# Reading the moving operand of the gate, value and output products from its last column to its first

## The chip, the cores and the metric

The kernel runs on one core of one Trainium2 chip. The metric is the device time of one execution in microseconds (us), the median of several runs. A change of 0.2% is 1.5 us here.

## The reference

An attention through 32 packed queries per head feeds a gated feed-forward layer. Eight batches of 576 positions, eight heads of 64, model width 512, inner width 1536; all data are float32.

```python
def sm_attn(qq, kk, vv):
    s = scale * np.matmul(qq, kk.transpose(0, 1, 3, 2))
    s = s - np.max(s, axis=-1, keepdims=True)
    a = np.exp(s)
    a = a / (np.sum(a, axis=-1, keepdims=True) + 1e-09)
    return np.matmul(a, vv)
p_packed = sm_attn(p, k, v)          # 32 rows per head
out = sm_attn(q, p_packed, p_packed) # 576 rows per head
...
x = out.transpose(0, 2, 1, 3).reshape(B * S, H * D)
g = x @ w_gate
silu = g * (1.0 / (1.0 + np.exp(-g)))
val = x @ w_val
return silu * val @ w_out
```

## The kernel before

**Stages.** For each batch `b` the first attention gives the 32 packed rows per head (`s1_...` for the first two batches, `q_...` from the third), the second attention gives the softmax weights of the 576 queries over the 32 packed rows (`s2_...`). The attention output itself is never formed. The packed rows are multiplied into the two weight matrices instead (`m_mm`, through `by_head` at L267), and the result, tile `m`, holds for one pair of 128-column blocks of the inner width what 128 (head, packed row) pairs contribute. The softmax weights stand transposed in tile `a2`: 128 partitions, two groups of heads, 576 query columns.

**Gate and value.** `gv_chunk` (L621) makes one block `fc` (0 to 11) of 128 inner columns for one chunk of queries. A batch has two chunks, A of 256 queries (`NA`) and B of 320 (`NB`); in even batches A comes first in the columns of `a2`, in odd batches B does. The stationary operand of each product is a 128x128 slice of `m`, the moving operand is the chunk's columns of `a2`, and the result in PSUM (tile `gv`) has the inner columns on partitions and the queries in its 256 or 320 columns. Both operands are split into a high and a low part in the type float32r, so that each product is three matmuls (low x high, high x low, high x high) for two head groups: six for the gate (`s` = 0), six for the value (`s` = 1), at L635.

**Output.** ScalarE takes the gate through SiLU (L642), VectorE multiplies it with the value (L646; the 64 queries of a chunk B beyond 256 go to tile `t4` at L649), and the product is split again into `hh` and `hl` (L178, L616). `out_mm` (L652) then takes 128 of these queries as stationary operand and a 512-column block of `w_out` as moving operand, in three parts (`hl` x `wo_h`, `hh` x `wo_l`, `hh` x `wo_h`, L654), and adds over the twelve `fc` in four PSUM tiles `acc`. `emit_out` (L662) copies a finished tile to SBUF and stores it with a DMA on SP's queue. After an odd batch the rows gathered in `t4` run through the same products into a tile `aux` (`behind_p4`, L963).

**Batch 0.** It runs from a list of words written out by hand (`PROGRAM`), beside the conversion of the weights from their 64-bit form. Its gate and value products are at L787, its output products at L828. For the first two weight tiles (`PLAIN`) and the first five pairs of `w_out` (`SPLIT`) it uses plain float32 operands, with one matmul per product in the code; the profile shows each of these as two.

**Order.** The steps of the next batches' attention are put between the products by the tables `FIRST` and `LATER` (`plan_of`, L707): at each place `fill`, `behind` and `between` in `gv_chunk` and `outs` a few of them are issued. TensorE's own order is the order of the code. The host lays the inputs out before the launch: `heads_t` (L991) puts the queries of a batch and head one after another in the order in which they come, `wo` (L1007) holds rows of `w_out` as they are.

Of the kernel before, what the change touches and what calls it, by code (L numbers as in the profile page):

```python
# [20 lines left out]
B, H, S, D = 8, 8, 576, 64  # L21
NP = 32
DM, DF = 512, 1536
P = 128
NPAR, NHP = 2, 4
NFC = DF // P
# [6 lines left out]
NA, NB = 256, 320  # L33
# [99 lines left out]
def tile_pack_attention_swiglu(ctx: ExitStack, tc: tile.TileContext, qT, kT, v, vq, pT, wgv, wout, out):  # L133
# [69 lines left out]
    sts, wos, wo_h, wo_l = {}, {}, {}, {}  # L203
# [58 lines left out]
    def by_head(outs, lhs, rhs):  # L262

        for hp in range(NHP):
            for par in range(NPAR):
                r = slice(64 * par, 64 * par + 64)
                nc.tensor.matmul(outs[par][32 * hp : 32 * hp + 32], lhs(r, hp), rhs(r, hp), start=True, stop=True)  # L267
# [344 lines left out]
    def h_split(src, hi, lo, between=lambda: False, tag=""):  # L612
        hh, hl = (pool.tile([P, 256], F32R, tag=t + tag, bufs=2, name=t) if tag else h_tile(t) for t in ("hh", "hl"))
        copy(hi, hh, src)
        last = between()
        low = lo.tensor_tensor(hl, src, hh.bitcast(F32), op=ALU.subtract)  # L616
        if last:
            pin(low)
        return hh, hl

    def gv_chunk(b, fc, is_b, fill, behind, between):  # L621
        odd = b % 2
        n = NB if is_b else NA
        off = (0 if odd else 256) if is_b else (320 if odd else 0)
        mh, ml = ms[b, fc // 2]
        ah, al = a2[b]
        f = fc % 2
        pgs = []
        for s in range(2):
            pg = ps_gv.tile([P, 512], F32, tag="gv", name="gv")  # L630
            pgs.append(pg)
            i = 0
            for m_, a_ in ((ml, ah), (mh, al), (mh, ah)):
                for g in range(NPAR):
                    nc.tensor.matmul(  # L635
                        pg[:, :n], m_[:, g, f, s * P : (s + 1) * P], a_[:, g, off : off + n],
                        start=(i == 0), stop=(i == 5),
                    )
                    i += 1
            fill()  # L640
        sg = pool.tile([P, NB], F32, tag="sg", bufs=1, name="sg")
        nc.scalar.activation(sg[:, :n], pgs[0][:, :n], AF.Silu)  # L642
        behind()
        hf = pool.tile([P, 256], F32, tag="hf", bufs=2, name="hf")
        o, o4 = (64, 0) if is_b and odd else (0, 256)
        nc.vector.tensor_tensor(hf, pgs[1][:, o : o + 256], sg[:, o : o + 256], op=ALU.mult)  # L646
        if is_b:
            r, r4 = slice(64 * odd, 64 * odd + 64), slice(o4, o4 + 64)
            nc.vector.tensor_tensor(t4[b // 2][:, fc, r], pgs[1][:, r4], sg[:, r4], op=ALU.mult)  # L649
        return h_split(hf, nc.scalar, nc.vector, between)  # L650

    def out_mm(acc, hh, hl, c, fc):  # L652
        for i, (h_, w_) in enumerate(((hl, wo_h), (hh, wo_l), (hh, wo_h))):
            nc.tensor.matmul(  # L654
                acc[:, :],
                h_[:, c : c + P],
                w_[fc // 2][:, fc % 2],
                start=(fc == 0 and i == 0),
                stop=(fc == NFC - 1 and i == 2),
            )  # L660
# [60 lines left out]
    with tc.manual_schedule(engines={mybir.EngineType.PE}):  # L721
# [17 lines left out]
        with tc.manual_schedule(  # L739
# [18 lines left out]
            rows, accs = [], []  # L758
# [13 lines left out]
            held = {}  # L772

            def gv(i):
                fc, is_b = order[i]
                off, n = (NA, NB) if is_b else (0, NA)
                k, f = divmod(fc, 2)
                if k < PLAIN:
                    terms = ((ms[0, k][0], a2fs[0]),)
                else:  # L780
                    (mh, ml), (ah, al) = ms[0, k], a2[0]
                    terms = ((mh, ah), (mh, al), (ml, ah))
                held[i] = [ps_gv.tile([P, 512], F32, tag="gv", name="gv") for _ in range(2)]
                for s in range(2):
                    todo = [(m_, a_, g) for m_, a_ in terms for g in range(NPAR)]
                    for j, (m_, a_, g) in enumerate(todo):
                        nc.tensor.matmul(  # L787
                            held[i][s][:, :n], m_[:, g, f, s * P : (s + 1) * P], a_[:, g, off : off + n],
                            start=(j == 0), stop=(j == len(todo) - 1),
                        )  # L790

            def half(i):
                fc, is_b = order[i]
                if fc // 2 < SPLIT:
                    return h0[fc // 2][:, fc % 2, 256 * is_b : 256 * is_b + 256]
                if i not in hs:
                    hs[i] = [pool.tile([P, 256], F32, tag="hf", bufs=2, name="hf")]
                return hs[i][0]
# [23 lines left out]
            def outs(i):  # L822
                fc, is_b = order[i]
                for c in range(2):
                    if fc // 2 >= SPLIT:
                        out_mm(accs[2 * is_b + c], *hs[i][1:], c * P, fc)
                        continue
                    nc.tensor.matmul(  # L828
                        accs[2 * is_b + c], half(i)[:, c * P : c * P + P], wos[fc // 2][:, fc % 2],
                        start=(fc == 0), stop=(fc == NFC - 1),  # L830
                    )

# [23 lines left out]
            def half_of(f, b):  # L856
# [5 lines left out]

            words = {
                "g": gv, "silu": silu, "h": hmul, "hh": h_high, "hl": h_low, "out": outs,
                "z_scores": lambda x: (None if x else s1_tile(0), s1_scores(0, x)), "z_max": lambda x: s1_max(0, x),
                "z_top": lambda x: s1_top(0), "z_exp": lambda x: s1_exp(0, True), "z_turn": lambda x: s1_turn(0, x),
# [26 lines left out]
        def last_outs(rows, accs, out):  # L893
# [5 lines left out]
            return last  # L899

        behind = last_outs(rows, accs, lambda which: outs(2 * NFC - 2 + which))

        steady[0] = True
        def batch(b, behind):
# [6 lines left out]
            def outs(fc, which, fill=lambda: None):  # L911
                src = (hb if which else ha).pop(fc)
                for c in range(2):
                    out_mm(accs[2 * which + c], *src, c * P, fc)
                    fill()

            for fc in range(NFC):
                count = [0]

                def fill():  # L920
                    count[0] += 1
                    if count[0] == 2:
                        run(fc, 2)
                        if fc == NFC - 1 and b + 1 < B:
                            m_part(b + 1, 0, both)
                        elif fc % 2 and fc + 1 < NFC:
                            m_part(b, (fc + 1) // 2, both)
                    if b == 1 and 1 <= fc <= 2 * SPLIT - 4 and count[0] == 7:
                        wout_high(fc + 3)
                        wout_low(fc + 3)  # L930
                    if count[0] != 2:
                        run(fc, count[0])

                ha[fc] = gv_chunk(b, fc, False, fill, lambda: run(fc, "a"), lambda: run(fc, "ha"))
                m_lows()
                if fc:
                    outs(fc - 1, 0, fill)
                else:
                    behind(0)
                hb[fc] = gv_chunk(b, fc, True, fill, lambda: run(fc, "b"), lambda: run(fc, "hb"))  # L940
                if fc:
                    outs(fc - 1, 1, fill)
                else:
                    behind(1)
                    for x, y in zip((rows, accs), accs_of(b)):
                        x.extend(y)
# [11 lines left out]
            def mm4(*ks):  # L958
                for k in ks:
                    for i in range(2):  # L960
                        out_mm(p4[0], *halves[k], i * P, 2 * k + i)
# [59 lines left out]
```

## Time and profile before

| | |
|---|---|
| median of 3 runs | 735.83 us (735.49 to 736.95) |
| the profiled execution's own time | 736.46 us |
| its span, first to last instruction | 734.7 us |
| TensorE matmul (PE) busy | 725.7 us, 99% of the span |
| weight loads (PEld) busy | 592.0 us, 81% |
| VectorE (DVE) busy | 454.4 us, 62% |
| ScalarE (ACT) busy | 373.9 us, 51% |
| granted TensorE clock, mean | 0.998 |
| DMA, mean over the span | 81 GB/s |

PE's rows are matmuls, PEld's rows the weight loads, which run beside them. A matmul's own duration contains its way through the array, so the durations of successive matmuls overlap. What one matmul costs a stream is therefore the distance from its start to the next one's start. The chain of waits follows the work that ended last back from the last instruction; a row of it in order of time has a start, a stretch in us, the engine, the tile and line, and how many instructions the stretch holds. For a piece with nothing but matmuls in a row, the stretch divided by the count is that distance. Rows of the timeline have start, length, engine, line, operation, operands and shape; equal neighbours are merged, with their count at the end.

### The profile page before, as it was taken

Reading aid. Unit: us, or ns where it says so; the run is one execution under the profiler, and the core shown is the slowest. Engines: PE = TensorE matmul, PEld = TensorE weight load, DVE = VectorE, ACT = ScalarE, POOL = GpSimd, SP = SyncE. Lnnn points to the kernel's source line nnn. Section 1 sums busy time; section 2 is a strip of 40 time slices with the busy share of each in tenths; the row PEclk is TensorE's granted clock in tenths of the full one; section 3 lists DMA queues with packets and bytes.
Section 4 is the critical chain, followed back from the end, with each engine's and each line's share of the span. In section 5 each row is a group of like instructions: output and inputs, shape, how many; then the busy total and the mean of one; then the engine's idle time right before and its main releaser. Section 6 shows DMA issues by size and latency. Waiting matters only on the chain.

```text
span 734.7 us, 15099 instructions
## 1 busy us (share of the span) xinstructions
PE 725.7 (99%) x6242; PEld 592.0 (81%) x6242; DVE 454.4 (62%) x1009; ACT 373.9 (51%) x668; POOL 2.0 (0%) x13
## 2 busy tenths in 40 slices
PE   8999999999999999999999999999999999999997
PEld 4655667888888888888888888888888888888886
DVE  4999779665755557663764646665574555744333
ACT  3789737754635445563563535654453535533331
POOL 0000000000000000000000000000000000000000
PEclk9999999999999999999999999999999999999999
DMA  9697482310112201302112011102001000010001
GB/s 351 249 356 269 145 308 97 117 73 2 65 58 85 74 1 65 127 4 73 66 44 98 15 63 65 40 22 73 1 2 72 4 2 1 1 58 1 1 1 71
DMA packets 20004, 59.15 MB, mean 81 GB/s; under 512 B 5984, under 2 KB 7008, under 8 KB 17376
## 3 DMA queue, kind: packets, MB, share of 16 engines
q1 hardware_dynamic: 19792, 58.12, 21.8%
q8 instruction: 49, 0.80, 0.4%
q14 instruction: 19, 0.16, 0.1%
q10 hardware_dynamic: 144, 0.07, 0.0%
HBM read 48.69 MB, written 9.49 MB: 79 GB/s over the span
## 4 chain that ended last, share of the span: by engine, by line
PE 95%; DVE 1%; issue 0%; DVEq 0%
PE gv L635 36%; PE acc L654 33%; PE aux L267 7%; PE gv L787 6%; PE acc L828 5%; PE aux L654 4%; PE gv_aux L482 1%; PE gv_aux L398 1%; PE gv_aux L267 1%; DVE w L200 0%; PE acc L728 0%; PE aux L343 0%; DVE e L467 0%; DVE w L201 0%; PE aux L324 0%
## 5 line engine op out<-in xcount | busy, mean ns | idle before, releaser
L642 ACT ACTIVATE sg<-gv 128x256 f32<-128x256 f32 (+1 forms) x168 | 69.1, 411 | 176.0 <-PE gv L635 162.0
L646 DVE TENSOR_TENSOR hf<-gv,sg 128x256 f32<-128x256 f32 x168 | 71.0, 423 | 130.2 <-PE gv L635 118.9
L635 PE MATMUL gv<-a2h,ml 128*128 128x256 f32 (+1 forms) x672 | 143.9, 295 | 0.0
L635 PE MATMUL gv<-a2l,mh 128*128 128x256 f32 (+1 forms) x672 | 143.5, 295 | 0.0
L635 PE MATMUL gv<-a2h,mh 128*128 128x256 f32 (+1 forms) x672 | 143.3, 294 | 0.0
L654 PE MATMUL acc<-wo_h,hl 128*128 128x512 f32 x344 | 140.7, 409 | 0.0
L654 PE MATMUL acc<-wo_h,hh 128*128 128x512 f32 x344 | 135.4, 394 | 0.0
L654 PE MATMUL acc<-wo_l,hh 128*128 128x512 f32 x344 | 134.8, 392 | 0.0
L635 PEld LDWEIGHTS gv<-a2h,ml 128*128 128x128 f32 x672 | 116.4, 188 | 15.1 <-ACT sg L803 0.4
L178 ACT CAST hh<-hf 128x256 fp32r<-128x256 f32 x168 | 67.8, 403 | 102.0 <-DVE hf L646 101.9
L635 PEld LDWEIGHTS gv<-a2l,mh 128*128 128x128 f32 x672 | 107.8, 188 | 0.0
L635 PEld LDWEIGHTS gv<-a2h,mh 128*128 128x128 f32 x672 | 107.7, 188 | 0.0
L616 DVE TENSOR_TENSOR hl<-hf,hh 128x256 fp32r<-128x256 f32 x168 | 69.9, 416 | 46.5 <-ACT hh L178 46.4
L654 PEld LDWEIGHTS acc<-wo_h,hl 128*128 128x128 f32 x344 | 64.5, 187 | 27.8 <-issue 19.2
L654 PEld LDWEIGHTS acc<-wo_h,hh 128*128 128x128 f32 x344 | 64.5, 188 | 15.5
L654 PEld LDWEIGHTS acc<-wo_l,hh 128*128 128x128 f32 x344 | 64.7, 188 | 8.1 <-issue 0.2
L569 DVE TENSOR_TENSOR ml<-aux,mh 128x512 fp32r<-128x512 f32 x92 | 59.0, 682 | 5.6 <-ACT mh L599 5.5
L267 PE MATMUL aux<-w,ppt 64*32 64x512 f32 (+1 forms) x784 | 52.1, 588 | 0.9 <-DVE w L201 0.9
L599 ACT CAST mh<-aux 128x512 fp32r<-128x512 f32 x92 | 49.4, 590 | 5.7 <-PE aux L267 1.3
L642 ACT ACT_TABLE_LOAD x30 | 38.5, 1283 | 13.8 <-PE gv L635 10.0
L828 PE MATMUL acc<-wo_f,h 128*128 128x512 f32 x80 | 37.8, 603 | 0.0
L828 PEld LDWEIGHTS acc<-wo_f,h 128*128 128x128 f32 x80 | 14.2, 189 | 16.6 <-issue 16.2
(153 smaller groups left out, 756.6 us busy)
## 6 DMA issues: line engine op xcount, KB each, us to landing
st<-in_wgv SPq DMA_DIRECT2D x12, 1024.0 KB, 5.8
k_t<-in_kT SPq DMA_DIRECT2D x16, 576.0 KB, 4.9
q_t<-in_qT SPq DMA_DIRECT2D x16, 576.0 KB, 4.9
out<-ot SPq DMA_DIRECT2D x36, 256.0 KB, 2.1
v_t<-in_vq SPq DMA_DIRECT2D x6, 1280.0 KB, 5.7
st<-in_wout SPq DMA_DIRECT2D x6, 1024.0 KB, 6.0
v_t<-in_v SPq DMA_DIRECT2D x2, 1024.0 KB, 8.5
p_t<-in_pT SPq DMA_DIRECT2D x7, 64.0 KB, 2.4
```

The lines of the kernel that those rows point to most:

```text
L178: e.copy(dst, src)
L267: nc.tensor.matmul(outs[par][32 * hp : 32 * hp + 32], lhs(r, hp), rhs(r, hp), start=True, stop=True)
L398: nc.tensor.matmul(pss[par][NP * j : NP * j + NP, i * SQ : (i + 1) * SQ], p_t[r, 2 * g + i, :], k_t[r, j // 2, 2 * g + i, j % 2 * SQ : j % ...
L569: pin(nc.vector.tensor_tensor(*lows.pop(0), op=ALU.subtract))
L599: nc.scalar.copy(m[0][at], src)
L616: low = lo.tensor_tensor(hl, src, hh.bitcast(F32), op=ALU.subtract)
L635: nc.tensor.matmul(pg[:, :n], m_[:, g, f, s * P : (s + 1) * P], a_[:, g, off : off + n], start=(i == 0), stop=(i == 5),)
L642: nc.scalar.activation(sg[:, :n], pgs[0][:, :n], AF.Silu)
L646: nc.vector.tensor_tensor(hf, pgs[1][:, o : o + 256], sg[:, o : o + 256], op=ALU.mult)
L654: nc.tensor.matmul(acc[:, :], h_[:, c : c + P], w_[fc // 2][:, fc % 2], start=(fc == 0 and i == 0), stop=(fc == NFC - 1 and i == 2),)
L787: nc.tensor.matmul(held[i][s][:, :n], m_[:, g, f, s * P : (s + 1) * P], a_[:, g, off : off + n], start=(j == 0), stop=(j == len(todo) - 1),)
L828: nc.tensor.matmul(accs[2 * is_b + c], half(i)[:, c * P : c * P + P], wos[fc // 2][:, fc % 2], start=(fc == 0), stop=(fc == NFC - 1),)
```

## The change

A helper `back_to_front` takes an access pattern with one run of columns and returns one that starts at the last column and steps backward by one. It is applied to the moving operand at all four places where the feed-forward products are issued: L635, L654 (L658 in the changed program), L787 (L791) and L828 (L832). The stationary operands and the PSUM tiles keep their patterns. So that the results come out in the same columns, the host lays two inputs out backward: the columns of `w_out`, and the queries of each chunk, so that `a2` holds a chunk's queries in reverse. The host's work is not part of the time.

```diff
-                        pg[:, :n], m_[:, g, f, s * P : (s + 1) * P], a_[:, g, off : off + n],
+                        pg[:, :n], m_[:, g, f, s * P : (s + 1) * P], back_to_front(a_[:, g, off : off + n]),
...
+    def back_to_front(x):
+        (p0, pn), (step, n) = x.ap
+        return bass.AP(x.tensor, x.offset + (n - 1) * step, [(p0, pn), (-step, n)])
+
     def out_mm(acc, hh, hl, c, fc):
...
-                w_[fc // 2][:, fc % 2],
+                back_to_front(w_[fc // 2][:, fc % 2]),
...
-                            held[i][s][:, :n], m_[:, g, f, s * P : (s + 1) * P], a_[:, g, off : off + n],
+                            held[i][s][:, :n], m_[:, g, f, s * P : (s + 1) * P], back_to_front(a_[:, g, off : off + n]),
...
-                        accs[2 * is_b + c], half(i)[:, c * P : c * P + P], wos[fc // 2][:, fc % 2],
+                        accs[2 * is_b + c], half(i)[:, c * P : c * P + P], back_to_front(wos[fc // 2][:, fc % 2]),
...
-    qT, kT = heads_t(q), heads_t(k)
+    backward = [
+        np.r_[n - 1 : -1 : -1, S - 1 : n - 1 : -1] for b in range(B) for n in ((NB if b % 2 else NA),)
+    ]
+    qT, kT = heads_t(np.stack([q[b][:, backward[b]] for b in range(B)])), heads_t(k)
...
-    wo = np.ascontiguousarray(wo).reshape(NFC, P, DM).view(np.int64)
+    wo = np.ascontiguousarray(wo[:, ::-1]).reshape(NFC, P, DM).view(np.int64)
```

The order of the instructions on every engine, their shapes and the semaphores they wait for are the same in both programs, row by row; only the line numbers differ. Of a moving operand only the first address and the sign of the step change: for one product of chunk B the pattern goes from 320 columns from column 256 upward to 320 columns from column 575 downward.

## The prediction

> **What bounds the kernel now.** I read the profile's page first, for which engine is busy and what the chain of waits is made of.
>
> ```profile
> span 734.7 us, 15099 instructions
> PE 725.7 (99%) x6242; PEld 592.0 (81%) x6242; DVE 454.4 (62%) x1009; ACT 373.9 (51%) x668; POOL 2.0 (0%) x13
> PE 95%; DVE 1%; issue 0%; DVEq 0%
> PE gv L635 36%; PE acc L654 33%; PE aux L267 7%; PE gv L787 6%; PE acc L828 5%; PE aux L654 4%; PE gv_aux L482 1%; PE gv_aux L398 1%; PE gv_aux L267 1%; DVE w L200 0%; PE acc L728 0%; PE aux L343 0%; DVE e L467 0%; DVE w L201 0%; PE aux L324 0%
> ```
>
> The chain runs through matmuls for 95% of the span, and 84% of it (36 + 33 + 6 + 5 + 4) is the five groups whose moving operand the change turns round. VectorE and ScalarE stand at 62% and 51%: a few per cent more or less on TensorE passes to the end nearly whole. How often the groups run is in the groups of matmuls with the shapes kept apart, here the three parts of the output products and one gate and value row of each shape (the two other operand pairs have the same counts).
>
> ```profile
> L654 PE MATMUL acc<-wo_h,hl 128*128 128x512 f32 x344 | 140.7, 409 | 0.0
> L654 PE MATMUL acc<-wo_h,hh 128*128 128x512 f32 x344 | 135.4, 394 | 0.0
> L654 PE MATMUL acc<-wo_l,hh 128*128 128x512 f32 x344 | 134.8, 392 | 0.0
> L654 PE MATMUL aux<-wo_h,hl 128*128 128x512 f32 x48 | 18.8, 391 | 0.0
> L635 PE MATMUL gv<-a2h,ml 128*128 128x320 f32 x336 | 76.8, 309 | 0.0
> L635 PE MATMUL gv<-a2h,ml 128*128 128x256 f32 x336 | 67.1, 281 | 0.0
> ```
>
> So 3 x 336 = 1008 products of 256 columns, 1008 of 320, and 3 x (344 + 48) = 1176 of 512: 258,048 + 322,560 + 602,112 = 1,182,720 moving columns in float32r. The mean durations in these rows overlap from one matmul to the next, so the cost of one is taken from the chain in order of time: start, stretch, what, count. First batch 0 with plain float32, then the steady stage, then the tail.
>
> ```profile
> 45.34 2.15 PE gv L787 x8
> 50.00 1.73 PE gv L787 x8
> 55.10 5.15 PE acc L828 x12
> ...
> 655.56 1.42 PE gv L635 x12
> 656.99 1.39 PE acc L654 x6
> 658.38 1.76 PE gv L635 x12
> ...
> 722.74 8.17 PE aux L654 x36
> ```
>
> Divided by the counts: plain float32 takes 2150 / 8 = 269 ns, 1730 / 8 = 216 ns and 5150 / 12 = 429 ns, the last for 512 columns. The timeline tells which shapes the gate and value stretches hold.
>
> ```profile
> 49.84 1.89 PE L787 MATMUL gv<-a2f,mh 128*128 128x256 f32 x8
> ...
> 52.68 2.42 PE L787 MATMUL gv<-a2f,mh 128*128 128x320 f32 x8
> ...
> 655.40 0.40 PE L635 MATMUL gv<-a2h,ml 128*128 128x256 f32 x2
> ```
>
> 216 ns is thus 256 columns, and 269 ns fits 320: (429 - 216) / 256 = 0.832 ns per column and 3 ns per matmul, and 320 x 0.832 + 3 = 269. In float32r the same division gives 1420 / 12 = 118.3 ns for 256 columns, 1760 / 12 = 146.7 for the other chunk's 320, and 1390 / 6 = 231.7 for 512. The slope is (146.7 - 118.3) / 64 = 0.443 ns per column and, from 320 to 512, (231.7 - 146.7) / 192 = 0.443 again; 118.3 - 256 x 0.443 leaves 4.9 ns per matmul. Two things are to be seen. Float32r takes 0.443 ns per column, where half of plain float32's 0.832 would be 0.416: 0.027 ns per column is lost. And the 4.9 ns per matmul is not owed: in the tail 36 products in a row take 8170 / 36 = 226.9 ns each, which is 512 x 0.443 = 226.8 and nothing besides.
>
> **The change part by part.** The added code issues no instruction and takes none away. Order, shapes and waits on each engine stay; DMAs keep their count, bytes and queue, since the host alone lays `q` and `w_out` out anew, which isn't timed. No wait is added, so nothing is queued behind one, and no cover is lost. The results land in the same PSUM columns in the same order of writing, so SiLU (L642), the multiplications (L646, L649), the splits and the stores see the tiles they saw. Each of these edits costs 0, without a range: they have no counterpart on the chip.
>
> What is left is one property: 1,182,720 float32r columns, and those of batch 0, are read at falling addresses. No trace here shows a matmul with a step of -1, so its price is bounded from both sides by the nearest rows.
>
> From above: the slowest rate at which a moving operand of full height is seen to pass is plain float32's 0.832 ns per column. If a falling read of float32r went at that, it would cost (0.832 - 0.443) x 1,182,720 = 460 us more. A nearer bound is that the 0.027 ns per column doubles: 0.027 x 1,182,720 = 32 us more. From below: if the 4.9 ns per matmul went in the 2016 gate and value products and the 1032 output products that aren't in the tail's kind of stretch, 3048 x 4.9 = 14.9 us would go; if the 0.027 ns went too, another 32 us.
>
> I take 0 for it. The loss has the size of a per-column rate that three shapes, two operands (`a2` and `w_out`) and two stages share to the third digit, as a limit does that counts columns or the bytes passed and not the direction. A run of 256, 320 or 512 columns covers the same addresses either way, ends where it began and holds as many words. Batch 0's plain matmuls have 0.416 ns per column to spare before a loss of that size would show at all. That gives 736.46 + 0 = 736.5 us for the profiled execution, which is 0.63 above the median of the three runs; on the median's scale it is 735.8 us.
>
> [...] In the chain 118.3 ns pass for 256 columns while a weight load of 128 columns runs beside each matmul:
>
> ```profile
> L635 PEld LDWEIGHTS gv<-a2h,ml 128*128 128x128 f32 x672 | 116.4, 188 | 15.1 <-ACT sg L803 0.4 <-ACT sg L642 0.3
> ```
>
> [...]
>
> **The rivals.**
>
> Faster: the 4.9 ns are collisions between the moving read and the weight load inside SBUF, and these depend on which addresses the two reads touch at the same moment. Both now rise; with one falling they would cross quickly instead of running along beside each other. For it: the loss comes and goes with the stretch, none in the tail, 4.8 ns (231.7 - 226.9) in the same products of the steady stage, where nothing but the neighbours in the stream is different, so something in the pairing of the reads makes it. Against it: the tail shows that two rising reads can run without it. If all of it goes, 735.8 - 14.9 = 720.9 us; if half, 728.4 us. VectorE and ScalarE have the room to follow.
>
> Slower, the other side: the reader of the moving operand is made for rising addresses, and a falling step costs it more per column, at L635 and L658 alike. Its place is every product of the steady stage; it decides from an extra 1.5 us / 1,182,720 columns = 0.0013 ns per column, a twentieth of the loss that is there. For it: float32r runs at the edge of what the read gives (0.443 against 0.416), so there is no slack to hide even a small extra, while plain float32 has some. Against it: nothing in the trace shows a reader that prefers a direction, all reads of the program being rising. At a third of the present loss it is +10.6 us, 746.4 us; at the whole of it 767.8 us; at plain float32's rate 1196 us.
>
> The change does nothing: this is the forecast itself, and it would look the same if the pattern were turned back into a rising one on the way to the chip; the operands that the trace records for L635 would tell.
>
> **How the numbers follow.** No change within 1.5 us (0.2%, about what a measurement of this kernel can tell from none): 0.38. Faster: 0.36, most of it between a tenth and the whole of the 14.9 us, with 0.04 for more than that. Slower: 0.26, since an unseen operand form without slack is a risk: 0.17 up to half of the doubled loss (+16 us, 752), 0.09 beyond, up to 1196 us. The likeliest case gives 735.8 us; its own range is 734.3 to 737.3. The range for all cases runs from 720, just beyond the whole gain, to 752: it leaves out 0.04 below and 0.09 above.
>
> **What would show it.** Right: the chain's stretches keep 1.42, 1.39 and 1.76 us for 12, 6 and 12 matmuls and 8.17 us for the tail's 36. The faster rival: the 6 products of L658 come to 6 x 226.9 = 1.36 us and the 12 of L635 to 1.36 and 1.70 us, with the tail unchanged. The slower rival: the tail grows too, by the same share per column as the steady stage, and the slope between 256, 320 and 512 columns rises above 0.443 ns while batch 0's 0.832 stays. Wrong altogether: a new wait in the chain on VectorE, ScalarE or a DMA, or a difference in the small attention products (L267, L398, L482), which the change leaves as they are.

## The result, and the profile after

| | before | after |
|---|---|---|
| median | 735.66 us (4 runs, 735.35 to 736.95) | 739.72 us (4 runs, 739.33 to 740.08) |
| the profiled execution's own time | 736.46 us | 739.33 us |
| its span | 734.7 us | 737.5 us |
| granted TensorE clock, mean | 0.998 | 1.000 |

The change makes the kernel slower, by 4.06 us between the medians: the ratio of the runs is 1.0054, with a 95% interval of 1.0042 to 1.0066. The page of the changed kernel has as many instructions on each engine, and the same lines make up the chain.

```profile
PE 728.2 (99%) x6242; PEld 591.9 (80%) x6242; DVE 454.6 (62%) x1009; ACT 373.6 (51%) x668; POOL 2.0 (0%) x13
PE 96%; DVE 1%; issue 0%; DVEq 0%
PE gv L635 36%; PE acc L658 34%; PE aux L267 7%; PE gv L791 5%; PE acc L832 5%; PE aux L658 5%; PE gv_aux L482 1%; PE gv_aux L398 1%; PE gv_aux L267 1%; DVE w L200 0%; PE acc L732 0%; PE aux L343 0%; DVE w L201 0%; PE aux L324 0%; DVE ot L180 0%; PE aux L398 0%
```

PE's busy time grows by 2.5 us, from 725.7; VectorE and ScalarE stay within 0.3 us, and no new engine, line or transfer has as much as 1% of the chain. The loss is inside the matmuls. Their own durations are no measure of it: in the rows of before they are some 162 ns longer than the distance from one to the next at each of the three shapes (281 ns beside 118.3, 309 beside 146.7, 394 beside 231.7). Which of them, the chain in order of time tells (start, stretch, what, count): batch 0 in plain float32, a stretch of 24 `aux` products, three stretches of the steady stage, the last 18 output products and the tail.

```profile
44.45 2.15 PE gv L791 x8
49.10 1.73 PE gv L791 x8
54.20 5.15 PE acc L832 x12
...
558.31 5.60 PE aux L658 x24
...
656.43 1.41 PE acc L658 x6
657.84 1.42 PE gv L635 x12
...
660.66 1.76 PE gv L635 x12
...
721.17 4.20 PE acc L658 x18
725.37 8.41 PE aux L658 x36
```

Two rows of before, for the same stretch of 24 and the last 18 output products:

```profile
556.69 5.45 PE aux L654 x24
...
718.63 4.12 PE acc L654 x18
```

Gate and value stand nearly where they stood, at 1.42 and 1.76 us for twelve; so does batch 0, with 2.15, 1.73 and 5.15. The float32r output products grew: six from 1.39 to 1.41 us, eighteen from 4.12 to 4.20, the tail's 36 from 8.17 to 8.41, which is 226.9 to 233.6 ns each. Over the whole chain, the 158 stretches of six that it holds whole sum to 228.01 us before and 229.94 after, 0.0122 us more for each. The program has 160 of these, which makes 2.0 us. Four stretches of 18 with 0.065 more each make 0.3. The `aux` products come four times 36 at a time: the tail has 0.24 us more, and three times they run as 24 and 12, with 5.60 after 5.45 and 2.81 after 2.76, 0.20 more each time; that makes 0.8. The stretches of twelve gate and value products, taken the same way, come to 1.419 us after 1.414 (256 columns) and 1.763 after 1.762 (320), 0.4 us at 84 of each. Together this is 3.5 us.

The two executions whose rows are shown differ by only 2.87 us (739.33 and 736.46), because the one of before was already 0.9 us late in batch 0: the same stretch starts at 45.34 us there and at 44.45 in the changed kernel. Its granted clock was 0.96 up to there, beside 1.00 in the other. Without that delay the difference is 3.8 us, and the stretches account for nearly all of it.

### The profile page after: what moved, and what is told of

It is laid out like the page before. It is cut to its first block, busy times and chain, and to the rows that moved or that the text cites. A ratio compares the mean times of both kernels' runs of the same rounds, so it can differ in the third digit from the quotient of the medians.

```text
span 737.5 us, 15099 instructions
## 1 busy us (share of the span) xinstructions
PE 728.2 (99%) x6242; PEld 591.9 (80%) x6242; DVE 454.6 (62%) x1009; ACT 373.6 (51%) x668; POOL 2.0 (0%) x13
## 4 chain that ended last, share of the span: by engine, by line
PE 96%; DVE 1%; issue 0%; DVEq 0%
PE gv L635 36%; PE acc L658 34%; PE aux L267 7%; PE gv L791 5%; PE acc L832 5%; PE aux L658 5%; PE gv_aux L482 1%; PE gv_aux L398 1%; PE gv_aux L267 1%; DVE w L200 0%; PE acc L732 0%; PE aux L343 0%; DVE w L201 0%; PE aux L324 0%; DVE ot L180 0%; PE aux L398 0%
## 5 line engine op out<-in xcount | busy, mean ns | idle before, releaser
L635 PE MATMUL gv<-a2h,ml 128*128 128x256 f32 (+1 forms) x672 | 144.2, 296 | 0.0
L635 PE MATMUL gv<-a2l,mh 128*128 128x256 f32 (+1 forms) x672 | 144.0, 296 | 0.0
L635 PE MATMUL gv<-a2h,mh 128*128 128x256 f32 (+1 forms) x672 | 144.0, 296 | 0.0
L658 PE MATMUL acc<-wo_h,hl 128*128 128x512 f32 x344 | 141.6, 411 | 0.0
L658 PE MATMUL acc<-wo_l,hh 128*128 128x512 f32 x344 | 136.8, 398 | 0.0
L658 PE MATMUL acc<-wo_h,hh 128*128 128x512 f32 x344 | 136.7, 397 | 0.0
L635 PEld LDWEIGHTS gv<-a2h,ml 128*128 128x128 f32 x672 | 116.6, 188 | 16.1 <-ACT sg L807 0.4
L635 PEld LDWEIGHTS gv<-a2l,mh 128*128 128x128 f32 x672 | 107.9, 188 | 0.0
L635 PEld LDWEIGHTS gv<-a2h,mh 128*128 128x128 f32 x672 | 107.7, 188 | 0.0
L658 PEld LDWEIGHTS acc<-wo_h,hl 128*128 128x128 f32 x344 | 64.6, 188 | 28.2 <-issue 19.2
L658 PEld LDWEIGHTS acc<-wo_h,hh 128*128 128x128 f32 x344 | 64.7, 188 | 15.7
L658 PEld LDWEIGHTS acc<-wo_l,hh 128*128 128x128 f32 x344 | 64.7, 188 | 8.3 <-issue 0.2
L832 PE MATMUL acc<-wo_f,h 128*128 128x512 f32 x80 | 37.8, 603 | 0.0
L832 PEld LDWEIGHTS acc<-wo_f,h 128*128 128x128 f32 x80 | 14.2, 189 | 16.6 <-issue 16.2
```

What stands on the lines that cost most here:

```text
L635: nc.tensor.matmul(pg[:, :n], m_[:, g, f, s * P : (s + 1) * P], back_to_front(a_[:, g, off : off + n]), start=(i == 0), stop=(i == 5),)
L658: nc.tensor.matmul(acc[:, :], h_[:, c : c + P], back_to_front(w_[fc // 2][:, fc % 2]), start=(fc == 0 and i == 0), stop=(fc == NFC - 1 and ...
L832: nc.tensor.matmul(accs[2 * is_b + c], half(i)[:, c * P : c * P + P], back_to_front(wos[fc // 2][:, fc % 2]), start=(fc == 0), stop=(fc == ...
```

## The experiments

**Which products.** The theory after the result: a falling read costs the output products something, and the gate and value products nothing. The rival: both pay, and the gate and value products hide it behind a gain. Two kernels do one half of the change each; the diffs are against the changed kernel.

```diff
# out_only: back_to_front at L658 and L832 and w_out's columns reversed; the queries stay in order
-  pg[:, :n], m_[...], back_to_front(a_[:, g, off : off + n]),
+  pg[:, :n], m_[...], a_[:, g, off : off + n],
...
# gv_only: back_to_front at L635 and L791 and the queries reversed; w_out stays in order
-  back_to_front(w_[fc // 2][:, fc % 2]),
+  w_[fc // 2][:, fc % 2],
...
```

> Only the output products read w_out back to front; the gate and value products read a2 forward as before. Pairing theory (what changed is how the moving read of an output product meets the weight load beside it): the whole change, 739.7 us against 735.7, since the trace after shows the 512-column products at about 233 to 234 ns and the 256- and 320-column ones as before. Direction theory (a falling step costs a fixed share per column wherever it is): the output products hold 602,112 of the 1,182,720 columns, so about half, 737.7 us.

> Only the gate and value products read a2 back to front; w_out is read forward. Pairing theory: 735.7 us, within 0.5 us of the kernel before, 118 and 147 ns per product. Direction theory: the other half of the columns, about 737.7 us.

The chain's last two stretches, first with the output products alone turned round, then with gate and value alone:

```profile
721.79 4.20 PE acc L658 x18
725.99 8.41 PE aux L658 x36
```

```profile
717.96 4.09 PE acc L658 x18
722.05 8.17 PE aux L658 x36
```

`out_only` takes 739.04 us beside 735.49 for the kernel before, ratio 1.0043 (1.0029 to 1.0056). `gv_only` takes 735.77, ratio 0.9997 (0.9989 to 1.0006). The output products carry the loss. But neither theory holds as put, since something small is hidden in the other half: over the chain of `gv_only`, twelve products of 256 columns take 1.425 us where they took 1.414, 0.9 us at 84 of them, while the forward output products gain about as much, six going from 1.443 to 1.436 on the mean (1.1 us at 160) and the last eighteen from 4.12 to 4.09. Why the output products gain there was not tried.

**One shape at a time.** The next kernel holds nothing but streams of 24 float32r products in a row on one moving operand and two alternating slices of a weight tile, 48 instructions for plain float32. In each pair one stream reads forward (up) and one back to front (down), at various distances in bytes. Distance 0 means that both reads start at the first column of their tiles, which are separate; any other distance moves the weights on by so many bytes (or, in one pair, the moving operand).

```python
for i in range(COUNT):
    nc.tensor.matmul(ps[:, :n], w[:, wo + 256 * (i % 2) : wo + 256 * (i % 2) + P],
                     run(m, mo, n, step), start=(i == 0), stop=(i == COUNT - 1))
```

> No part of the reference: 36 streams of 24 matmuls each, one after another, on one float32r moving tile and two float32r weight slices, with nothing beside them but weight loads. Names with up read the moving tile forward, with down back to front; the letter is the distance in address between weights and moving tile (a 0 bytes, b 256, c 32, d 64, e 128, f 16, g 4, i 96, j 512, k 48; h moves the moving tile by 32 bytes); short has 256 columns, mid 320, the others 512; plain is float32. Pairing theory: up_b, the tail's distance, takes 226.9 ns per matmul and down_b about 233.3; other distances give other values in both directions, and down is not slower than up at all of them. Direction theory: every down is slower than its up by about 6 ns at 512 columns, 3 to 4 at 256 and 320, whatever the distance; both theories: plain 429 ns in both directions.

The chain in order of time; `a` is distance 0, `up_c` 32 bytes, `up_j` 512 bytes, all of 512 columns; `short` is 256 columns, `mid` 320, `plain` 512 in float32:

```profile
14.94 5.44 PE up_a L81 x24
20.38 5.60 PE down_a L81 x24
...
37.05 5.60 PE up_c L81 x24
42.65 5.61 PE down_c L81 x24
...
115.54 5.46 PE up_j L81 x24
...
154.93 3.52 PE mid_up_a L81 x24
158.45 3.52 PE mid_down_a L81 x24
...
169.02 20.60 PE plain_up L81 x48
189.62 20.60 PE plain_down L81 x48
```

Two times for the same product are to be seen: 5440 / 24 = 226.7 ns and 5600 / 24 = 233.3 ns. The forward read has 226.7 to 227.5 only at distances 0, 256 and 512 bytes and 232 to 234 at the eight others; the falling read has 233 or more everywhere. 320 columns take 146.7 ns both ways, and plain float32 doesn't tell the directions apart (20600 / 48 = 429.2 ns both ways). These two times agree with the 226.9 and 233.6 of the kernel's tail.

**Is it the distance?** That suggested a simpler theory: what counts is how the two reads meet, and turning one round only spoils a good meeting. Then a forward read at a bad distance should cost the kernel as much as the change. One padding moves the weights of the output products by 64 bytes, to 192 from a multiple of 256:

```diff
-PAD = 120
+PAD = 104
```

> The kernel before, all reads forward, with the tiles after pp moved down by 64 bytes, so that the weights of an output product lie 192 bytes off a multiple of 256 from its w_out columns instead of on one; nothing else changes. Pairing theory: the same loss as the change without turning any read, the tail at 233.3 instead of 226.9 ns, 738.5 to 739.5 us. Theory that only the falling step costs (at these addresses or anywhere): no change, 735.5 us.

```profile
555.61 5.60 PE aux L654 x24
...
721.76 8.25 PE aux L654 x36
```

It takes 736.10 us beside 735.45, ratio 1.0005 (0.9996 to 1.0014). The three stretches of 24 `aux` products do go to 5.60 us, 233.3 ns a product, which is the falling read's time with every read forward; so the distance can take the better time away in the kernel too. But the tail goes only to 229.2 ns, the stretches of six stay (1.442 us on the mean after 1.443), and the kernel's time moves by 1.0 us at most by the interval: the distance alone is not the cause of the 4 us. That theory fell.

**Does anything give the falling read the better time?** Narrower weights (96, 64 and 32 columns, so that less is read beside the moving operand) and fifteen more distances:

> No part of the reference: streams of 24 matmuls as before. First 512 moving columns with weights of 128, 96, 64 and 32 columns (full, three, half, quarter), forward and back to front, at distance 0; the same with 320 (mid) and 256 (short) moving columns; then back to front with full weights at 15 further distances (down_), and forward at 192, 240, 384 and 512 bytes (up_). Pairing theory: the cost beyond 0.416 ns per column comes from the weight load beside the matmul, so it shrinks with the weight columns: from 233.3 for full to about 225 for half and 220 for quarter back to front. Theory that a falling read costs per column: back to front stays 6.6 ns above forward at all widths. If there is a distance at which the falling read meets no weights, one of the down_ rows shows about 226.7; if not, all show 233.

```profile
14.35 5.44 PE full_up L81 x24
19.79 5.61 PE full_down L81 x24
...
47.66 5.55 PE quarter_up L81 x24
53.21 5.60 PE quarter_down L81 x24
...
78.38 2.72 PE quarter_up_short L81 x24
81.10 2.83 PE quarter_down_short L81 x24
```

The falling 512 columns stay at 233.3 to 236.7 ns at all four widths and all fifteen distances. 256 columns read forward reach 2720 / 24 = 113.3 ns beside narrow weights and 117.9 falling. For 512 columns narrow weights work the other way: the forward read goes from 226.7 ns to 230 or 231. So the falling read's time is its own, while the forward read has a better one that it reaches only at times.

The weights have a part in a forward product's time: over the streams 512 columns take 226.7 to 227.5 or 232 to 234 ns with the weights at different distances, and 256 columns take 113.3 ns beside 32 weight columns where the next run has 2870 / 24 = 119.6 ns beside 128 at the same distance.

**Where 256 and 320 columns have their better time.** If the theory holds for these too, there is a distance at which they gain:

> No part of the reference: streams of 24 matmuls of 256 moving columns, forward (up_) and back to front (down_), with the weights at distances of 0, 16, 32 ... 240 bytes (letters a to p) and of 4 bytes (q). Pairing theory: values between 113 and 121 ns that depend on the distance, with neither direction ahead on average, which is why the gate and value products did not change. Theory that a falling read costs per column: each down_ about 3 ns above its up_.

> Streams of 24 float32r products with no part of the reference: 320 columns read forward at the sixteen distances 0, 16, ... 240 bytes (mod 256) between weights and moving operand (mid_a to mid_p), 256 columns at distances around 64 bytes and at 64 plus one, two, three and four times 256, a few falling ones. Theory A (the rising read has a best rate of 0.4427 ns per column, 226.7 / 512, which it reaches only at favourable distances; the falling read has its own, slower one everywhere): at one or more distances the 320-column stream takes near 320 x 0.4427 = 141.7 ns, at all others 146 to 148; the 256-column stream takes 113.3 at 64 + 256k for every k and 117 to 120 beside it; falling streams 146.8 and 117.8 at every distance, the favourable ones too. Theory B (the 113.3 ns of 256 columns at 64 bytes is a chance of its place in the program, and the fixed 4.9 ns a product are paid by both directions): 320 columns 146 to 148 at all sixteen distances, and 256 columns 117 to 120 at 64 + 256k as well.

In the first kernel `up_a` is distance 0 and `up_e` 64 bytes, 256 columns; in the second `short_c` is 64 bytes and `short_j` 1088 bytes, and `up_again` is `short_c` once more, behind falling streams.

```profile
11.73 2.87 PE up_a L81 x24
...
23.11 2.72 PE up_e L81 x24
```

```profile
73.35 2.74 PE short_c L81 x24
...
92.77 2.72 PE short_j L81 x24
...
118.06 2.83 PE up_again L81 x24
```

256 columns take 113.3 to 114.2 ns, at the least 256 x 0.4427, at 64 bytes and at 64 plus one to four times 256, and 116.7 to 120.4 elsewhere; falling 117.9 to 120.0 at every distance tried. 320 columns stay within 145.8 to 146.7 at all sixteen, so their part of the theory missed. (In `widths` they came to 143.8 forward, beside 32 weight columns.) `up_again` misses too: 117.9 ns at the good distance. So the distance alone doesn't fix a forward read's time; what came before may count too, but no run tries this by itself.

**The good distance in the kernel.** Paddings put every gate and value product 64 bytes from its moving operand, forward and, in a second kernel, with the whole change:

```diff
-                pool.tile([P, NPAR * 4 * P + 24], dt, tag=t, bufs=2, name=t)[:, at : at + NPAR * 4 * P].rearrange(
+                pool.tile([P, NPAR * 4 * P], dt, tag=t, bufs=2, name=t).rearrange(
...
-            t4[b // 2] = pool.tile([P, NFC, P], F32, tag="t4", bufs=1, name="t4")
+            t4[b // 2] = pool.tile([P, NFC * P + 48], F32, tag="t4", ...)[:, : NFC * P].rearrange(...)
...
-        sg = pool.tile([P, NB], F32, tag="sg", bufs=1, name="sg")
+        sg = pool.tile([P, NB + 16], F32, tag="sg", bufs=1, name="sg")[:, :NB]
```

> The kernel before, all reads forward, with the tiles moved by paddings: every float32r gate/value product now has its weights 64 bytes (mod 256) from the start of its moving operand (42 + 84 at the groups' edges 192), where they were spread over thirteen distances; the 869 + 137 out products that stood at distance 0 stay there. Theory A (a rising read reaches its own best rate at the favourable distance, in the kernel as in the streams): the 1058 products of 256 columns go from about 118.2 ns towards the 113.4 ns of the stream, at most 1058 x 4.8 ns = 5.1 us, less what each group of 12 needs to settle; the 1096 of 320 columns stay at 146.7: 731 to 734 us. Theory B (the distance decides only in long streams of one shape): 735.5, as before.

> The same paddings under the changed kernel, all moving operands read back to front. Theory A (the falling read has a rate of its own and finds no favourable distance): 739.7 as without the paddings, 256-column products still 117.6 to 118.5 ns; against the forward kernel with the same paddings the change then costs more than before, 6 to 9 us instead of 4. Theory C (the change costs time only because it alters the distance between the first column read and the weights, and a new distance can mend it): the gate/value products gain as in the forward kernel, 735 to 737.

Last two stretches of the forward kernel, then of the one that reads back to front:

```profile
719.10 4.14 PE acc L656 x18
723.24 8.17 PE aux L656 x36
```

```profile
719.99 4.20 PE acc L660 x18
724.19 8.41 PE aux L660 x36
```

Both misses. Forward takes 736.98 us beside 735.46, ratio 1.0017 (1.0008 to 1.0026): twelve 256-column products went only from 1.414 to 1.408 us where 1.36 was hoped for, and the last eighteen output products, which weren't meant to change, from 4.12 to 4.14, and six of them from 1.443 to 1.448 on the mean, 0.7 us at 160; the rest of the 1.5 us is not accounted for. Back to front takes 738.35, ratio 1.0036 (1.0022 to 1.0050), 1.4 us above its forward twin and 1.4 below the changed kernel. In this kernel's short runs of changing operands the good times of the long streams did not come about: 1408 / 12 = 117.3 ns, where the stream has 113.3. What does carry over is that the falling products have 4.20 and 8.41 us in both layouts tried, while the last eighteen forward ones move between 4.09 and 4.14 from kernel to kernel (4.09 in `gv_only`, which has the layout of before), and the tail between 8.17 and 8.25.

**What in a falling read costs?** The step of -1 itself, or the order in which stretches of memory are visited? Streams of 512 columns read in other orders:

> Streams of 24 float32r products with no part of the reference. 512 columns at distance 0 (a) and 64 bytes (b), read with step 1, -1, 2, -2, in two rising halves in order and swapped, in rising fours and sixteens laid back to front, and in fours that each fall while the fours rise; then 64, 128, 192, 384 and 448 columns with step 1 and -1. Theory A1 (it is the falling step itself): step 2 and all forms whose inner step rises by 1 take 226.7 ns at distance 0, -1, -2 and the falling fours 233.4. Theory A2 (any read that is not one run of adjacent rising columns loses the best rate): step 2, the fours and the sixteens take 233 or more too, only the halves in order stay at 226.7. On the lengths: if the falling read costs per column, 64/128/192/384/448 columns take near 30.5/59.3/88.2/175.1/204.1 ns (a line through 117.6 ns at 256 and 233.4 at 512); if it costs a fixed time per product on top of 0.4427 ns a column, they take 33 to 35, 61 to 63, 90 to 92, 175 to 177 and 203 to 205.

The chain at distance 0: `two` has step 2; `halves_swapped` reads columns 256 to 511, then 0 to 255; `quads_swapped` reads 508 to 511, 504 to 507 and so on; `quads_turned` 3, 2, 1, 0, 7, 6 and so on:

```profile
19.70 5.61 PE back_a L80 x24
25.31 10.83 PE two_a L80 x24
...
52.78 5.44 PE halves_swapped_a L80 x24
58.22 5.60 PE quads_swapped_a L80 x24
63.82 5.46 PE quads_turned_a L80 x24
```

Neither theory as put. The fours that fall inside, with three steps of -1 out of four, cost next to nothing (5460 / 24 = 227.5 ns beside 226.7); the fours that rise inside but come in falling order cost the whole price, 233.3 ns. In these streams the price is for walking to lower addresses from one 16-byte piece to the next. At 64 bytes none of these orders has the better time: all with steps of 1 or -1 take 233 to 235 ns, rising or not. The lengths of 64 to 192 columns can't be read: TensorE's granted clock fell in most of them (last section).

**The same in the kernel.** Two kernels change only the output products, with `w_out` laid out to match:

```diff
# out_fours_turned
+        return bass.AP(x.tensor, x.offset + (3) * step, [(p0, pn), (4 * step, n // 4), (-step, 4)])
# out_fours_swapped
+        return bass.AP(x.tensor, x.offset + (n - 4) * step, [(p0, pn), (-4 * step, n // 4), (step, 4)])
```

> Only the out products' moving operand is changed: w_out's columns lie turned within each group of four (16 bytes), and a product reads 3, 2, 1, 0, 7, 6, 5, 4, ...: three of four steps fall by one column, while the fours come in rising order. Theory D (what costs is the walk to lower addresses from one stretch of some 16 to 64 bytes to the next, not the falling step from column to column): 735.5, within 0.2% of the kernel before, the tail's 36 products near 8.17 us (226.9 ns each), out products on the mean 230 to 232 ns. Theory A1 (the falling step itself): 738 to 739, tail near 8.40 us.

> Only the out products' moving operand is changed: w_out's fours of columns lie in reverse order, and a product reads 508 to 511, 504 to 507, ...: three of four steps rise by one column, while the fours come in falling order. Theory D (the walk to lower addresses): 738.5 to 739.5, slower than the kernel before by 0.4 to 0.6% like the full reversal of the out products (739.04), tail near 8.40 us (233.4 ns each), no out product in its steady stretch below 231 ns. Theory A1 (the falling step from column to column): 735.5 to 736.5, tail near 8.2 us.

The tails, turned and swapped:

```profile
721.97 8.17 PE aux L658 x36
```

```profile
724.87 8.41 PE aux L658 x36
```

Turned: 735.93 us beside 735.62, ratio 1.0004 (0.9995 to 1.0013). Swapped: 739.46, ratio 1.0050 (1.0036 to 1.0064). Both as the walk to lower addresses has it; the falling step by itself is ruled out.

**From which size on.** Blocks of 2, 4, 8, ... 256 columns (letters a to h), laid back to front and each read rising (`swapped`), or in order and each read falling (`turned`):

> Streams of 24 float32r products of 512 columns at distance 0, with no part of the reference. swapped_a to swapped_h: blocks of 2, 4, 8, 16, 32, 64, 128 and 256 columns laid back to front, each read rising; turned_a to turned_h: blocks of the same sizes in rising order, each read falling. Theory D1 (each step to a lower address beyond a 64-byte stretch costs the same): swapped 233.4 ns up to 16 columns, then falling towards 226.7 by half for each doubling (230.0, 228.4, 227.5, 227.1, 226.9); turned 226.7 up to 16 columns, then 230.0 at 32, 231.7 at 64, rising to 233.4. Theory D2 (a wider stretch, say 1 KB, within which the order doesn't matter): swapped 233.4 up to 128 columns and 226.7 only at 256, turned 226.7 up to 128 or 256. Then 288 to 480 columns at distance 0 (up), 128 bytes (up_far) and falling (down): if the falling read costs per column its times lie on the line 117.6 ns at 256, 233.4 at 512 (132.1, 161.0, 175.5, 190.0, 204.4, 218.9), if by a fixed time on top of 0.4427 ns a column, 6.7 ns above 127.5, 155.8, 170.0, 184.2, 198.3, 212.5.

```profile
30.68 5.46 PE turned_b L80 x24
...
41.75 5.60 PE turned_c L80 x24
...
52.95 6.40 PE turned_d L80 x24
59.35 5.58 PE swapped_e L80 x24
...
70.62 5.46 PE swapped_f L80 x24
```

Turned blocks are free up to 4 columns (16 bytes, 227.5 ns) and cost from 8 (32 bytes, 233.3 ns) on; swapped blocks cost up to 32 columns (128 bytes, 232.5 ns) and are free from 64 (256 bytes, 227.5 ns) on. There is no sliding from one to the other, as a price for each step down would have it. The simplest reading is that a read has the better time open to it if its 16-byte pieces rise within each 256 bytes, and that the order of these stretches doesn't matter. Another fits as well, and no run parts the two: the price is full from some number of steps down to a lower piece on, between 7 in 512 columns (`swapped_f`, free) and 15 (`swapped_e`, 232.5 ns). On the lengths the run fits neither line: at 288 and 352 columns the falling stream's 133.3 and 162.5 ns lie between them, at 384, 416, 448 and 480 its 177.9, 191.2, 206.7 and 220.0 lie above both, and no forward stream has 0.4427 ns a column (131.7 ns at 288, 217.1 at 480).

**The change without its price.** If that is the cause, the changed kernel needs only its output products read in blocks of 64:

```diff
+        return bass.AP(x.tensor, x.offset + (n - 64) * step, [(p0, pn), (-64 * step, n // 64), (step, 64)])
...
-                back_to_front(w_[fc // 2][:, fc % 2]),
+                blocks_back_to_front(w_[fc // 2][:, fc % 2]),
...
-    wo = np.ascontiguousarray(wo[:, ::-1])...
+    wo = np.ascontiguousarray(wo.reshape(NFC * P, DM // 64, 64)[:, ::-1])...
```

> The changed kernel, with one difference: the out products' moving operand is read in blocks of 64 columns (256 bytes) laid back to front, each block rising, and w_out's columns are laid out to match; the gate/value products still fall column by column. Theory D (the price is for the order of 16-byte pieces within 256 bytes): the loss goes, 735.4 to 736.4, within 0.2% of the kernel before, tail near 8.17 us. If the streams' threshold does not carry over to the kernel: 738 to 739.7, tail 8.40 us.

```profile
722.68 8.17 PE aux L662 x36
```

735.76 us beside 735.86, ratio 1.0000 (0.9991 to 1.0009). The whole loss is gone, with everything else of the change in place.

## Why the prediction was wrong

- **What bounds the kernel**: right. The chain is PE at 96%, and what the matmuls lost came to the end nearly whole: 3.1 + 0.4 us by the stretches, 3.8 between the two executions from batch 0 on.
- **The edits that cost nothing** (PSUM, SiLU, splits, stores, the host's layouts): right. VectorE and ScalarE are within 0.3 us of before, and `after_blocks_64` keeps all these edits at 1.0000.
- **The price of the falling read, the step that failed**: "I take 0 for it. The loss has the size of a per-column rate that three shapes, two operands (`a2` and `w_out`) and two stages share to the third digit, as a limit does that counts columns or the bytes passed and not the direction." That step put the output products' falling read at nothing, and it costs 3.1 us there by the stretches. The rate does not count columns alone: the tail's 512 columns take 8410 / 36 = 233.6 or 8170 / 36 = 226.9 ns by the order in which 16-byte pieces are visited (`out_fours_swapped` against `out_fours_turned`, 739.46 against 735.93 us). The sentence behind it, that a run "covers the same addresses either way", is true and proves nothing.
- **The common slope was partly chance.** It was drawn through two kinds of product. By the streams, 118.3 ns for 256 columns is the slower kind, whose better one is 113.3; 226.9 in the tail is the better kind of 512; 231.7 in the steady stage lies between 226.7 and 233.4. So what was read as 4.9 ns "per matmul" that the tail does without looks, by the streams, like the distance between the two kinds.
- **The bounds looked past the nearest row.** The prediction saw that the tail's 226.9 ns had no such 4.9 ns and asked only who could gain by losing them. Read the other way, products that already had the better time could lose it: for the 144 products of the tail's kind 144 x 4.8 ns = 0.7 us, from the prediction's own rows; they lost 0.8. The larger part, 2.3 us, is in the 1032 output products of the steady stage, some 2 ns in each; there the rows of before alone don't show that 231.7 ns is a mean that can still grow. The prediction's nearer bound upward, 32 us, came from doubling the 0.027 ns a column, and no row stood for the doubling; the 0.416 behind it, half of plain float32's rate, was the author's estimate, and the best float32r stream has 0.4427.
- **The slower rival**: right in sign, in the tail that grows, in batch 0 that stays and in the slope from 320 to 512 columns: (1402 / 6 - 146.9) / 192 = 0.452 ns after 0.443, from the mean of the chain's tighter stretches of six. The shares are not the same, as it had them: the tail's products grew by 6.7 ns, those of the steady stage by some 2. Wrong in "at L635 and L658 alike": in `gv_only` the gate and value products lost 0.9 us, which the output products behind them made good (0.9997). Wrong in its sizes, +10.6 us and more: products that already had the slower time, as 256 columns with 118.3 ns, had little more to lose.
- **The faster rival**: partly borne out. By the streams, where the weights lie has a part in which of the two times a forward read gets (226.7 to 227.5 ns at three distances, 232 to 234 at eight); that the two reads collide was the author's guess and not shown. And turning the read round brought no better time: the falling read had 233 ns or more at every distance tried.

Left open: what inside the chip makes falling pieces slower; whether stretches of 256 bytes or the number of steps down decides; why the good distances repeat every 256 bytes; why a forward output product in the kernel has some 231 ns on the mean and not 226.7; and whether the price goes by the column or by the product. No kernel tried was faster than the kernel before.

## What to carry to other kernels

Where float32r matmuls of 512 columns bound a kernel, lay a moving operand out so that each 256 bytes of it are read upward; here reversing blocks of 64 columns was free (735.76 us beside 735.86), and so was turning columns within 16 bytes (735.93 beside 735.62), while the whole reversal cost 3.1 us in 1176 products. When one shape shows two times in a trace, take the distance between them as what a change can lose, not only as what it can gain, and count the products that have the better one. And the steady time of a long stream of one shape was no forecast for the short runs of changing operands here (113.3 ns in the stream, 117.3 in the kernel): measure that in the kernel.

## What else the runs showed of the hardware

512 columns with step 2 took twice the time of step 1: `two_a` has 10830 / 24 = 451 ns where step 1 has 226.7.

The slowest order of the same 512 columns was blocks of 16 (64 bytes), each read falling, the blocks in rising order: `turned_d` has 6400 / 24 = 266.7 ns, where the full reversal has 233.8 (`back_a`).

From 143 to 168 us of `steps`, in most of its streams of 64 to 192 columns, the granted clock was 0.51. The table by stretch: stretch, length, busy time and count on each engine, PEclk, DMA.

```profile
143.00:168.00 25.00, 25.00 (x120) 25.00 (x121) 3.53 (x9) 0.00 (x0) 0.00 (x0) 0.51 0.14 53
186.00:211.00 25.00, 25.00 (x119) 21.93 (x118) 3.12 (x5) 0.00 (x0) 0.00 (x0) 1.00 0.14 53
```

PE and the weight loads are both busy throughout in the first stretch, at a clock of 0.51; in the second, with 448 and 512 columns to a load, the loads have gaps and the clock stands at 1.00. The three streams of 192 columns show two times: the first takes 4920 / 24 = 205.0 ns a product, the last two, from 167.97 us on, 2680 / 24 = 111.7. What made the clock fall was not tried.
